# Left-key scores of four heads in one matmul, and a new unit order, in a two-branch attention kernel

## The chip, the cores and the metric

The kernel runs on one core of a Trainium2 chip, as one program. The metric is the time on the device in microseconds; the profile that is quoted comes from one profiled execution of the program.

## The reference, cut to what matters

The output mixes two attention branches of the same input `x` (2048 rows, 512 columns) by a gate of each row. Branch A goes through 64 segments of 32 rows, one after the other: each segment works on its 32 rows and 8 memory rows, and the first 8 rows of its result are the memory of the next segment. The 64 segments are therefore a serial chain. Branch B (`_B_ref`) has four blocks of 512 rows with causal attention inside each and a running memory; nothing in it depends on branch A.

```python
mem = mem0
for s in range(n_seg):                        # 64 segments of seg_len = 32
    xs = x[:, s*seg_len:(s+1)*seg_len, :]
    h = concatenate([mem, xs], axis=1)        # 8 + 32 = 40 rows
    q, k, v = (einsum('btd,dhe->bhte', h, W) for W in (Wq, Wk, Wv))   # 32 heads of 128
    scores = where(mask, einsum('bhqe,bhke->bhqk', q, k) * scale, -1e9)
    o = einsum('bhqk,bhke->bhqe', softmax(scores), v)
    o = einsum('bhte,hed->btd', o, Wo)
    mem = o[:, :M, :]                         # M = 8
    outs.append(o[:, M:, :])
g = sigmoid((x * gate_w).sum(-1))
return g * a + (1 - g) * b                    # a: branch A, b: branch B
```

## The kernel before

All work is recorded first as operations with their dependencies (class `Prog`) and then written out, engine by engine, in the order of recording; waits on semaphores are derived from the dependencies. Each engine thus runs its instructions strictly in the order in which they were recorded.

**Splitting of a segment.** A segment has 40 rows, handled as 32 "main" rows (8 memory rows and the first 24 of its own) and 8 "left" rows (its last 8). K, Q and V of the main rows are made for each segment. Those of the left rows do not depend on the chain and are made for four segments (a group) at once: units whose names begin with `L`. The 32 heads of a segment are handled in two halves, b = 0 and 1, of 16 heads. Within a half, four heads share each of four tiles j: tile j of 32 partitions holds the keys of heads 4j to 4j + 3 of the half, and these stand side by side along the columns. Each head has `LW` = 56 columns in the score bank: 40 for the main keys against all queries, then 16 for left keys against the queries that may see them (the 8 memory rows and the 8 left rows). The left keys of a tile's four heads, 8 each, fill its 32 partitions together (`KTL`); they are multiplied with the queries of all four heads, and the products of one head's keys with another's queries are masked away. `QT_sb` and `KTL` keep heads in pairs: the two members u of a pair are interleaved, element by element.

**The units of a segment**, in the names that the order uses (`s.` in front is the segment, b the half): `K0x K0y V0x ... Q1x Q1y` are projection passes of 8 matmuls of 512 columns (Q1: 16 of 256), `k q v` evacuate them from PSUM, `TK TQ` transpose K and Q on DVE, `qt` copies left queries on POOL, `Z` puts a mask into a score bank by a matmul (L1547), `S` computes scores (`scores`, L1551 to L1571), `X` takes exponentials on ACT (L1575), `Y` applies a mask on DVE, `M` makes the row sums by matmul (L1594), `L` turns them into reciprocals on ACT (L1601, L1604), `N n` multiply them in on DVE and POOL, `PV` multiplies with values (L1625 main, L1636 left), `E0` to `E3` evacuate (L383 on ACT, L385 on DVE), `W0` to `W3` are the out projection (L1362), `hm` turns the eight new memory rows into input of the next segment (L1662 to L1667), `H ws oL` evacuate and store the result.

**Other units.** `L` units make left K, Q, V of a group, `O` and `T` units finish the output rows of a group, `pj pp` project parts of branch B, and `bS bE bP bT` are its scores (L932), exponentials (L953), values (L985) and remaining steps.

**What sets the order.** The text `A_ORDER` (L1058 on) lists all 4509 units; `plan_a` calls them in that order. A `~` behind a unit swaps the engine that evacuates in it: ACT in place of DVE or the other way (`evac`, L383 and L385).

**The scores before.** After 16 matmuls for the main keys (L1561), two loops k and j make eight matmuls for the left keys (L1566): weights are the left keys of tile j (32 columns), moving are the queries of two of its four heads, 32 columns.

Of the kernel before, what the change touches and what calls it, by code (L numbers as in the profile page):

```python
# [867 lines left out]
class BAttn:  # L868
# [195 lines left out]
    1.TQ0 1.TQ1x 1.k1 1.S0~ 1.TK1 1.q1y 1.TQ1y 1.V0x bE 1.S1~ 1.X0 bE 1.X1 1.V0y~ 1.Y0 1.M0 1.v0 1.L0 1.V1x 1.M1 1.L1 1.N0 1.V1y 1.n0 1.n1 1.v1~ 1.N1 pj
    pj bE 1.PV~ 1.E0 1.E1~ L1.VL0x 1.E3 1.E2 bE 1.oL 1.W0 1.W1 1.W2 1.W3 pp~ 1.hm bS 1.H bP bP 2.qt L1.VL0y bE L1.VL0e pj bE 2.K0x 2.K0y~ bT 2.Q0x~ 2.Q0y~
    2.Q1x~ bE bE bP 2.k0 bP 2.TK0 bS 2.q0~ 2.q1x 2.TQ0 2.Q1y~ 2.q1y~ 2.K1x~ 2.TQ1x 2.TQ1y bE 2.K1y~ 2.S0 bE bE 2.X0 1.ws 2.k1~ 2.Z1 2.V1x pj bE 2.V1y~
    2.TK1 2.Y0 2.S1 2.v1 2.M0 pp 2.V0x 2.X1 3.qt bP 2.M1 bS~ bP 2.V0y 2.L0 2.N0 2.L1 2.n1 2.n0 2.N1 pj pj 2.v0 bT bE bE 2.PV pj bE 2.E0 2.W0 2.E1~ 2.E2~
    2.E3~ bE pp~ 2.W1 2.W2 2.W3 2.hm bP 2.H bP bS~ pj pj 3.K0x bE bE bE 3.K0y~ 3.Q0x 3.k0~ 3.Q0y~ 3.K1x bE 3.q0~ 2.ws 3.K1y~ 3.Q1x~ 3.Z1 3.TK0 3.k1 3.q1x
    3.TQ0 3.S0 3.Q1y pp~ 3.V0x~ 3.TK1 3.X0 3.Y0 3.TQ1x 3.q1y bP 3.TQ1y bP 3.M0 3.L0 pj 3.S1~ bS 3.X1 pp~ 3.V0y~ 3.M1 3.V1x~ 3.n0 bE 3.V1y bE 3.L1 3.v0 pj
    3.n1 3.N0 3.v1~ 2.oL bE 3.N1 pj 3.PV~ 3.E0~ L1.VL1x 4.qt 3.E1 L1.VL1y bE 3.W0 3.W1 3.E2 3.W2 3.E3~ 3.W3 L1.VL1e 3.hm pp 3.H bP pj bS~ bP pj L1.VLt  # L1070
    4.K0x bE 4.K0y 4.Q0x~ bT 4.Q0y~ bT bE bE bE 4.k0 4.Q1x~ 4.Q1y 3.ws L2.xl pp~ bP bP 4.K1x 4.TK0 4.q0~ 4.q1x~ 4.TQ0 4.K1y 4.q1y 4.S0 bS 4.TQ1x 4.TQ1y
    4.X0 4.V1x~ 4.k1~ 4.Z1 bE 4.V1y~ 4.TK1 3.oL 4.S1 bE 4.Y0 4.M0 bE 4.v1 4.X1 4.V0x~ 4.L0 4.V0y 4.v0 4.M1 4.L1 4.n0 pj pj 4.N0 4.N1 4.n1 pj 4.PV~ bE pj
    bP 4.E1 4.E0 4.E2~ 4.E3 4.W0 4.W1 4.W2 pp~ 4.W3 bS~ bP O0.0 bE pp~ 4.hm O0.1 5.K0x~ 5.K0y bE 5.Q0x 4.H 5.qt bT 5.k0~ 5.Q0y~ 5.K1x~ bE bE 5.K1y 5.TK0
    5.Z1 5.q0~ 5.TQ0 5.k1~ 5.Q1y 5.TK1 5.q1y 5.TQ1y 5.S0~ 5.X0 5.Q1x~ bP 5.V1x~ 5.q1x 5.V1y~ 4.ws 5.Y0 5.M0 5.TQ1x 5.v1 5.S1~ 5.V0x~ 5.X1 5.V0y~ 5.L0 5.M1
    5.v0 O0.2 5.L1 5.N0 4.oL 5.n0 O0.3 bP 5.N1 5.n1 5.PV L2.KL1x 5.E0~ L2.KL1y O0.e 5.E1~ bS~ O0.s 5.E2~ 5.E3 5.W0 5.W1 bE 5.W2 5.W3 L2.KL0x bE L2.KL1e
    L2.KL0y~ bE bE bS bP 5.hm 5.H 6.qt L2.KL0e~ bP 6.Q1x~ 6.K0x~ 6.Q0x 6.Q0y bE bE 6.K0y 6.q1x~ bE bE 6.Q1y~ 6.TQ1x 6.q0~ 5.oL bS bP bT bP 6.k0~ 6.q1y
    6.K1x~ 6.TQ0 bE 6.TK0 6.K1y~ 6.k1~ 6.S0~ bE bE 6.V1x 6.V1y~ 6.Z1 6.TQ1y 6.TK1 6.X0 6.V0x~ bE 5.ws 6.S1 6.Y0 6.M0 6.X1 6.v1 6.L0 6.V0y 6.M1 6.L1 bP bP
    6.v0 bS 6.n1 6.N0 6.N1 L2.QL1x 6.n0 bE L2.QL1y bE bT 6.PV bE 6.E0 6.E1 6.E2 L2.QL0x 6.E3~ 6.W0 L2.QL1e 6.W1 6.W2 bE 6.W3 bP 7.qt bS 7.Z1 6.hm 6.H bP
    bE L2.QL0y~ bT 7.Q1x~ bE 7.K0x~ 6.ws L2.QL0e 6.oL 7.Q0x~ 7.Q0y 7.K0y 7.q1x 7.TQ1x bE bE 7.K1x 7.k0 7.q0 7.TQ0 7.K1y 7.Q1y bP bP 7.k1 7.TK0 7.S0~ 7.TK1
    bS~ 7.q1y 7.X0 bE 7.V0x~ 7.TQ1y 7.Y0 7.S1~ 7.V0y 7.v0 bE 7.M0 7.V1x~ 7.X1 7.M1 7.L0 7.L1 7.V1y~ 7.N0 L2.VL0x 7.n0 7.v1 7.N1 L2.VL0y L2.VL1x 7.n1 bE  # L1080
    7.PV L2.VL1y bE L2.VL0e bP 7.E2 7.E0~ bT 7.E1~ L2.VL1e~ bP bS~ 7.W0 8.qt 7.E3 bE L2.VLt 7.W1 7.W2 7.W3 bE bE bE 7.hm 7.H bS~ 8.Z1 bP bP bE bT bE 8.Q0x
    bE 8.Q0y 8.q0 8.K0x 8.K0y 8.K1x bE 8.k0 8.K1y 8.k1 8.TQ0 8.Q1y 8.TK0 8.Q1x 8.S0 8.q1y 8.q1x 8.V1x~ 8.TK1 8.X0 8.TQ1y 8.V1y 8.TQ1x 8.Y0 8.S1~ L3.xl
    9.Z1 8.M0 bP 8.v1 8.V0x~ 8.X1 7.oL 8.L0 8.M1 8.L1 8.N0 8.V0y 8.N1 L3.KL1x 7.ws 8.v0~ O1.0 8.n0 8.n1 8.PV~ 8.E0 8.E1~ 8.E3~ L3.KL1y bP 8.E2~ 8.W0 8.W1
    8.W2 L3.KL1e 9.qt 8.W3 bS~ O1.1 bE bE O1.2 8.hm 9.Q0x~ 9.Q0y 8.oL bE bE 9.K0x~ 8.H 9.K0y 9.K1x~ 9.q0 9.K1y~ 9.k0~ 9.TQ0 9.Q1y~ 9.k1 9.q1y 9.TK0 9.Q1x~
    9.TK1 9.TQ1y 9.q1x 9.TQ1x 9.S0 9.X0 9.Y0 9.V1x 9.V1y~ 8.ws 9.S1~ bP 9.X1 9.M0 9.V0x~ 9.L0 9.M1 9.V0y 9.L1 L3.KL0x 9.v1 9.N0 9.n0 9.n1 9.v0~ L3.KL0y
    9.N1 9.PV O1.3 9.E0 bP O1.e 9.W0 9.E1 9.E2~ 9.W1 bT 9.W2 9.E3~ 9.W3 11.Z1 bS 9.hm 10.Z1 10.qt L3.KL0e~ L3.QL0x bE bE bE O1.s bT L3.QL0y~ 10.Q0x 10.K0x
    L3.QL0e 9.H 10.Q0y~ 10.K1x~ 10.q0 10.K0y 10.K1y~ bE 10.TQ0 10.Q1y~ 10.k0 10.Q1x 9.oL 10.TK0 10.k1 10.TK1 10.V1x 10.q1y 10.q1x 10.TQ1y 10.TQ1x 10.S0~
# [151 lines left out]
    T14.b 62.PV~ 62.E0 62.E2 62.W0 63.qt 62.E1 62.E3 62.W1 62.W2 62.oL 62.W3 O15.0 O15.1 62.hm O15.2 O15.3 63.Q0x 63.V0x T14.a 62.H O15.e 63.Q0y 63.K0x
    63.q0 63.K0y 63.TQ0 63.K1x 63.Q1y 63.K1y 63.k0 63.TK0 T14.t 63.S0 62.ws O15.s 63.Q1x~ 63.q1y~ 63.k1~ 63.X0 63.Y0 63.q1x 63.V1x~ 63.M0 T15.l 63.V0y~  # L1240
    63.TK1 63.V1y 63.TQ1x 63.TQ1y 63.S1~ 63.L0 63.v0 63.X1 63.v1~ 63.n0 63.M1 63.L1 T14.f 63.N0 63.n1 T15.b 63.N1 63.PV~ 63.E0 63.E1 63.E3 63.E2 T15.a
    63.W0 63.W1 63.W2 63.W3 T15.t 63.H T15.f
# [534 lines left out]
```

## Time and profile before

| | |
|---|---|
| median of three runs | 830.14 us (827.49 to 831.01) |
| profiled execution, its own time | 830.02 us |
| its span, first to last instruction | 828.3 us |
| TensorE busy (matmuls, lengths modelled) | 788.2 us, 95% |
| DVE, ACT, POOL busy | 71%, 68%, 35% |
| left-key matmuls (L1566) | 1024, mean length 177 ns |
| main-key score matmuls (L1561) | 2048, mean length 182 ns |

In the profile, PE is TensorE's matmuls and PEld its weight loads, which run beside them. Lengths of matmuls overlap, since they are pipelined: what a group of them takes from its successor is the distance from its start to the next group's start. An entry in brackets at a row's end is the time the engine had stood idle, with what released it.

### The profile page before, as it was taken

To read this page: it belongs to the slowest core of one execution; us is meant where nothing else is said; L and a number is where in the kernel's file an instruction comes from. 1 tells how busy PE (TensorE), PEld (TensorE's weight loads), DVE (VectorE), ACT (ScalarE), POOL (GpSimd) and SP (SyncE) were. 2 spreads that over 40 slices of the span, in tenths; PEclk is the share of its full clock that TensorE was granted. 3 is DMA by queue.
4 is the path that set the end of the run, shared out by engine and by line. 5 is a ranking of instruction groups with operands and counts; after the bars stand their busy time and mean duration, and the time that the engine had idled before them with its cause. 6 is when DMAs were issued, how large, how long until landed. Compare 5 with 4: busy or idle time off the path is not lost.

```text
span 828.3 us, 51528 instructions
## 1 busy us (share of the span) xinstructions
PE 788.2 (95%) x23213; PEld 485.5 (59%) x23219; DVE 591.1 (71%) x1483; ACT 560.0 (68%) x1356; POOL 289.1 (35%) x727
## 2 busy tenths in 40 slices
...
PEclk9999999999999999999999999999999999999999
...
DMA packets 100600, 72.34 MB, mean 87 GB/s; under 512 B 58036, under 2 KB 94492, under 8 KB 98844
## 3 DMA queue, kind: packets, MB, share of 16 engines
...
q8 instruction: 182, 2.98, 1.6%
...
## 4 chain that ended last, share of the span: by engine, by line
PE 80%; DVE 9%; ACT 7%; issue 2%; POOL 1%; DMA 0%; DVEq 0%; POOLq 0%
PE ps L1279 38%; PE ps L1362 15%; PE ps L1501 6%; PE ps L698 3%; PE ps L932 2%; PE ps L1625 2%; PE ps L985 2%; ACT PTT L953 2%; PE ps L1594 2%; PE ps L1561 2%; PE ps L1442 1%; DVE oTt L1009 1%; PE ps L717 1%; ACT R_sb L1604 1%; POOL PTT L959 1%
## 5 line engine op out<-in xcount | busy, mean ns | idle before, releaser
L953 ACT ACTIVATE PTT<-ps 128x512 bf16<-128x512 f32 x320 | 173.6, 604 | 49.6 <-PE ps L932 34.9
L959 POOL TENSOR_SCALAR_AFFINE_SELECT PTT<-PTT 128x128 bf16<-128x128 bf16 (+2 forms) x320 | 121.7, 380 | 217.7 <-ACT PTT L953 199.6
L1279 PE MATMUL ps<-Wv_sb,xTp 128*32 128x512 bf16 x2048 | 144.1, 379 | 0.0
L1279 PE MATMUL ps<-Wk_sb,xTp 128*32 128x512 bf16 x2048 | 133.3, 379 | 2.6 <-DVE xTp L1667 2.2
L1362 PE MATMUL ps<-Wo_sb,OT_sb 128*32 128x256 bf16 x4096 | 125.6, 273 | 7.6 <-ACT OT_sb L383 3.7
L1362 PEld LDWEIGHTS ps<-Wo_sb,OT_sb 128*32 128x32 bf16 x4096 | 103.5, 97 | 31.1 <-ACT OT_sb L383 21.8
L1613 POOL TENSOR_TENSOR P_sb<-P_sb,R_sb 128x64 bf16<-128x64 bf16 x128 | 49.9, 390 | 176.0 <-ACT R_sb L1604 171.6
L383 ACT ACTIVATE QN_sb<-ps 128x256 bf16<-128x256 f32 (+1 forms) x155 | 67.2, 439 | 34.0 <-PE ps L1279 29.5
L1279 PEld LDWEIGHTS ps<-Wk_sb,xTp 128*32 128x32 bf16 x2048 | 56.6, 97 | 50.5 <-DVE xTp L1667 7.8
L383 ACT ACTIVATE OT_sb<-ps 128x320 bf16<-128x320 f32 x167 | 62.9, 439 | 30.4 <-PE ps L1636 29.5
L383 ACT ACTIVATE KN_sb<-ps 128x512 bf16<-128x512 f32 x89 | 53.1, 600 | 32.9 <-PE ps L1279 32.6
L385 DVE CAST V_sb<-ps 128x512 bf16<-128x512 f32 x82 | 56.4, 688 | 25.7 <-PE ps L1279 24.0
L1501 PE MATMUL ps<-Wq_sb,xTp 128*32 128x256 bf16 x2048 | 72.0, 273 | 0.8 <-DVE xTp L1667 0.5
L1279 PE MATMUL ps<-Wq_sb,xTp 128*32 128x512 bf16 x1024 | 70.1, 380 | 2.5 <-DVE xTp L1667 2.1
L1291 DVE STREAM_TRANSPOSE QT_sb<-QN_sb 128x128 f32<-128x128 f32 (+1 forms) x192 | 63.0, 335 | 11.1 <-ACT QN_sb L383 9.1
L1291 DVE STREAM_TRANSPOSE KT_sb<-KN_sb 128x256 f32<-128x256 f32 x128 | 55.7, 435 | 14.7 <-ACT KN_sb L383 10.9
L1501 PEld LDWEIGHTS ps<-Wq_sb,xTp 128*32 128x32 bf16 x2048 | 54.4, 97 | 19.8 <-DVE xTp L1667 6.2
L1575 ACT ACTIVATE P_sb<-ps 128x224 bf16<-128x224 f32 x128 | 45.6, 358 | 28.9 <-PE ps L1566 23.6
L1662 DVE STREAM_TRANSPOSE tt<-ps 128x256 f32<-128x256 f32 x63 | 28.3, 449 | 44.2 <-PE ps L1362 43.5
L385 DVE CAST OT_sb<-ps 128x320 bf16<-128x320 f32 x89 | 40.2, 483 | 23.9 <-PE ps L1636 23.7
L1608 DVE TENSOR_TENSOR P_sb<-P_sb,R_sb 128x160 bf16<-128x160 bf16 x128 | 41.0, 331 | 15.8 <-ACT R_sb L1604 15.1
L1279 PEld LDWEIGHTS ps<-Wv_sb,xTp 128*32 128x32 bf16 x2048 | 44.6, 95 | 12.7 <-ACT KN_sb L383 0.7
...
## 6 DMA issues: line engine op xcount, KB each, us to landing
...
```

What stands on the lines that cost most here:

```text
L383: P.op("act", lambda a: a.activation(dst, src, ACT.Copy), reads=[v.rbank[k] for k in bks], writes=dres, name=name)
L385: P.op("dve", lambda d: d.tensor_copy(dst, src), reads=[v.rbank[k] for k in bks], writes=dres, name=name)
L953: P.op("act", lambda a: a.activation(pt, v.pb[bk], ACT.Exp, scale=v.SCALE_B), reads=[v.rbank[bk]], writes=[rp], name="be%d_%d" % (n, t))
L959: P.op("gp", lambda g: g.affine_select(mv, mv, [[0, len(cut)], [1, 128]], ALU.is_ge, 0.0, base=0, channel_multiplier=-1), reads=[rp], writ ...
L1279: ins = pe.matmul(pb[bk][SEG * j:SEG * (j + 1), :], lhs(c), cols(w, j) if split else w[:, 512 * j:512 * (j + 1)], start=(c == 0), stop=(c ...
L1291: P.op("dve", lambda d: d.transpose(to, src), reads=reads, writes=writes, name=name)
L1362: ins = pe.matmul(pb[bk][SEG * j:SEG * (j + 1), 0:256], lhs(h), Wo_sb[:, h, :].rearrange("p (k q c) -> p q k c", q=2, c=64)[:, j % 2], sta ...
L1501: ins = pe.matmul(pb[bk][SEG * j:SEG * (j + 1), 0:256], lhs(c), cols(w_sb[:, c, 2048 * b + 1024 * half:2048 * b + 1024 * (half + 1)], j), ...
L1575: P.op("act", lambda a: a.activation(P_sb[:, b, :], pb[bk][:, 0:So], ACT.Exp, scale=SCALE), reads=[rbank[bk]], writes=[Rs("Pm%d" % b), Rs( ...
L1608: P.op("dve", lambda d: d.tensor_tensor(wide[b][:, :, 0:L], wide[b][:, :, 0:L], R_sb[:, b, :].rearrange("p (i q) -> p i q", q=L), ALU.mult ...
L1613: P.op(ENG["n"], lambda d: d.tensor_tensor(left, left, grp04(R_sb[:, b, :]), ALU.mult), reads=[Rs("R0_%d" % b)], writes=[Rs("PL%d" % b)], ...
L1662: P.op("dve", lambda d: d.transpose(v.tt[:, :, :].rearrange("p (k n) t -> p k n t", n=2), src), reads=[rbank[wb["bk"]]], writes=[Rs("tt")] ...
```

## The change

Two things change. First, in `scores`, the loop over k goes: the left keys of tile j are multiplied with the queries of all four heads in one matmul of 64 columns, so a unit has four such matmuls in place of eight. The queries are now read in the order head pair, position, member of the pair (the two members of a pair are neighbours in `QT_sb`), and so the output is written in that order too: `p (k u w) -> p k w u` puts the member u, `LW` = 56 fp32 columns apart, innermost. Before, each matmul wrote two runs of 16 neighbours.

```diff
-                for k in range(2):
-                    for j in range(4):
-                        m = 8 * b + 2 * j
-                        ins = pe.matmul(heads4(pb[bk][SEG * j:SEG * (j + 1), 0:So])[:, 2 * k:2 * k + 2, L:LW], KTL[par][:, r, m // 2, :, :, :].rearrange("p k m u -> p (k m u)"),
-                                        QT_sb[:, m + k, :, :].rearrange("p (a q) u -> p u a q", q=8)[:, :, 0::4, :],
-                                        start=new, stop=True, skip_group_check=True)
+                for j in range(4):
+                    m = 8 * b + 2 * j
+                    lefts = pb[bk][SEG * j:SEG * (j + 1), 0:So].rearrange("p (k u w) -> p k w u", u=2, w=LW)[:, :, L:LW, :]
+                    ins = pe.matmul(lefts, KTL[par][:, r, m // 2, :, :, :].rearrange("p k m u -> p (k m u)"),
+                                    QT_sb[:, m:m + 2, :, :].rearrange("p k (a q) u -> p k a (q u)", q=8)[:, :, 0::4, :],
+                                    start=new, stop=True, skip_group_check=True)
```

Second, `A_ORDER` is another list of the same 4509 units; the number of each unit stays. Some `~` marks move as well. One line of it, from segment 0:

```diff
-    0.k0~ wl wl bP L1.xl L1.KL0x L1.KL1x 0.V1y~ L0.QL0e~ 0.TQ1x 0.Z1 wl 0.qt 0.S1~ wl 0.TK0 L1.KL1y~ 0.S0 0.v1~ L1.QL1x L1.KL0y~ L1.QL1y L0.VLt wl wl pp
+    0.k0~ wl wl bP L1.xl L1.KL0x L1.KL1x 0.V1y~ L0.QL0e~ 0.TQ1x 0.Z1 wl 0.qt 0.TK0 L1.KL1y L1.KL0y pj 0.S1 wl L0.VLt 0.X1 wl 0.S0 0.v1 L1.KL1e L1.KL0e~
```

Place one: TensorE in segment 0, from the last V pass to the row sums. L1547 is the mask, L1561 and L1566 are the scores of one half, L1594 the sums, `Wk_sb,xL` and `Wq_sb,xL` passes for left rows of group 1, L836 a pass of branch B. Before:

```order
L1279 MATMUL ps<-Wv_sb,xTp 32x512 x8
L1547 MATMUL ps<-mbias,id 32x224 x4
L1561 MATMUL ps<-QT_sb,KT_sb 32x40 x16
L1566 MATMUL ps<-QT_sb,KTL 32x2x16 x8
L1279 MATMUL ps<-Wk_sb,xL 32x512 x8
L1561 MATMUL ps<-QT_sb,KT_sb 32x40 x16
L1566 MATMUL ps<-QT_sb,KTL 32x2x16 x8
L1279 MATMUL ps<-Wq_sb,xL 32x512 x8
L1279 MATMUL ps<-Wk_sb,xL 32x512 x8
L1279 MATMUL ps<-Wq_sb,xL 32x512 x8
L1594 MATMUL ps<-P_sb,onesb 32x160 x4
```

The same place in the changed kernel:

```order
L1279 MATMUL ps<-Wv_sb,xTp 32x512 x8
L1547 MATMUL ps<-mbias,id 32x224 x4
L1279 MATMUL ps<-Wk_sb,xL 32x512 x16
L836 MATMUL ps<-woB_sb,xTp 32x512 x8
L1561 MATMUL ps<-QT_sb,KT_sb 32x40 x16
L1566 MATMUL ps<-QT_sb,KTL 32x2x16x2 x4
L1561 MATMUL ps<-QT_sb,KT_sb 32x40 x16
L1566 MATMUL ps<-QT_sb,KTL 32x2x16x2 x4
L1594 MATMUL ps<-P_sb,onesb 32x160 x4
```

Three passes now stand ahead of the first scores that stood behind them or further on; the two score groups follow each other, and the sums of the first come right behind. Left-key groups are four matmuls in place of eight.

Place two: TensorE in segment 19, from its last V pass over the values (L1625, L1636) to the out projection (L1362). L932 is a score step of branch B, L985 one of its value steps. Before:

```order
L1279 MATMUL ps<-Wv_sb,xTp 32x512 x8
L932 MATMUL ps<-KQj 128x256 x8
L1625 MATMUL ps<-P_sb,V_sb 128x40 x32
L1636 MATMUL ps<-P_sb,VL 128x4x2x8 x8
L1279 MATMUL ps<-Wk_sb,xL 32x512 x8
L1362 MATMUL ps<-Wo_sb,OT_sb 32x256 x64
L1279 MATMUL ps<-Wk_sb,xL 32x512 x8
```

In the changed kernel:

```order
L1594 MATMUL ps<-P_sb,onesb 32x160 x4
L1594 MATMUL ps<-P_sb,onesb 32x4x2x8 x4
L985 MATMUL ps<-PTT,Vj 32x256 x8
L932 MATMUL ps<-KQj 128x256 x8
L1625 MATMUL ps<-P_sb,V_sb 128x40 x32
L1636 MATMUL ps<-P_sb,VL 128x4x2x8 x8
L1362 MATMUL ps<-Wo_sb,OT_sb 32x256 x64
L1279 MATMUL ps<-Wk_sb,xL 32x512 x8
```

The projection pass for left rows between values and out projection has gone behind the out projection; a value step of branch B now stands ahead of the values in place of the last V pass, which lies one group earlier. Such moves run through the whole program.

More of the change, by code (lines that the diff above doesn't have):

```diff
@@ L1064 @@
[L1064 to L1087, printed above, removed]
@@ L1239 @@
[L1239 to L1242, printed above, removed]
+    15.k1 15.q1y 15.TK0 15.q1x 15.TK1 15.S0~ 15.V0x~ 15.X0 15.TQ1y 15.TQ1x 14.oL 15.V0y 15.Y0 15.S1~ bP 15.M0 15.X1 bP 15.V1x~ bT 15.M1 15.L0 15.L1 14.ws
@@ new lines @@
+    17.Z1 bE bE 17.Q0x~ bE 17.Q0y 17.K0x~ 17.K0y~ 17.q0~ 17.TQ0 17.K1x 17.k0~ 17.K1y~ 17.Q1x 17.TK0 T2.t 16.H~ bE 17.Q1y~ 17.k1 17.q1x 17.q1y 17.S0
+    17.V0x~ 17.TK1 17.TQ1x 17.X0 16.ws 17.TQ1y 17.V0y 17.S1~ 17.Y0 17.v0 bP 17.X1 17.M0 17.V1x 17.L0 17.M1 17.V1y 17.L1 L5.QL0x L5.QL0y~ 18.Z1 17.v1~
+    17.n0 17.N0 17.n1 17.N1 16.oL 17.PV~ bP L5.VL0x L5.QL0e 17.E0 17.E1~ 17.W0 17.W1 17.E3~ 17.E2~ 17.W2 bT 17.W3 17.hm O3.0 18.qt bT L5.VL0y O3.1 18.K0x
+    18.K0y~ 18.Q0x 18.Q0y~ 18.K1x L5.VL0e~ 18.K1y 18.k0~ 18.Q1x~ 18.TK0 18.q0~ 18.TQ0 18.k1 18.TK1 18.Q1y~ 18.S0~ 18.V1x 18.q1x 18.TQ1x 18.q1y 18.V1y~
@@ new lines @@
+    21.K1x~ 21.K1y~ 21.TQ0 21.Q1x bP 21.S0~ O4.e~ bP 21.k1 21.q1x O4.s bS 21.V1x 21.TK1 21.TQ1x 20.oL 21.Z1 21.X0 21.S1 bE 21.Y0 T2.f 21.M0 bE 21.X1
+    21.V1y 21.L0 21.V0x~ 21.M1 21.V0y 21.v1 21.n0 21.N0 21.L1 21.N1 21.v0~ 21.n1 L6.VL0x 21.PV bE 21.E3 L6.VL0y 21.E0 21.E2~ 21.W0 L6.VL0e 21.E1~ bE 21.W1
+    21.W2 21.W3 21.hm bS~ bP 22.qt bP 22.Z1 L6.QL0x 21.H 22.Q0x bE 22.K0x 22.Q0y 22.K0y~ bT bE 22.q0 bE bE 22.K1x 22.TQ0 22.k0 22.K1y~ 22.Q1y~ 22.TK0
+    22.Q1x~ 22.k1 22.q1y 22.q1x 22.S0 22.TK1 22.V0x 22.V1x~ 22.TQ1y 22.TQ1x 22.X0 22.S1 22.Y0 23.Z1 22.X1 22.M0 22.L0 22.V1y 22.v1 22.N0 21.oL 22.M1
@@ new lines @@
+    29.M0 28.ws 29.V0y 29.X1 29.v0 29.M1 29.L0 L8.QL0x 29.n0 29.N0 L8.QL0y bP 30.Z1 29.L1 29.n1 29.N1 29.PV L8.QL0e 29.E0 30.qt 29.E2~ 29.E1~ bT 29.W0
+    29.W1 29.E3~ 29.W2 29.W3 bS~ bP bE 29.hm O6.1 bE bE bE O6.2 30.K0x 30.K0y 30.k0 30.Q0x 30.TK0 30.Q0y 30.q0~ 30.TQ0 30.K1x~ 30.K1y 30.Q1x~ 30.Q1y~
+    30.k1 30.q1x 30.S0 30.V0x~ 30.q1y 30.V0y 30.TK1 30.X0 30.TQ1x 30.TQ1y 30.Y0 30.S1 29.oL 30.X1 30.M0 30.V1x~ 30.M1 30.v0 30.V1y L8.VL0x 30.L0 30.N0
+    30.n0 L8.VL0y 30.L1 30.n1 30.v1~ 30.N1 31.qt 30.PV O6.3 30.E0 30.E3 30.E1~ bP 30.W0 30.E2~ 30.W1 O6.e 30.W2 30.W3 L8.QL1x L8.VL1x L8.VL1y 31.Z1
@@ new lines @@
+    32.k1 32.S0 32.TK1 32.q1y 32.X0 32.TQ1y 32.V1x 32.V0x~ 32.S1~ 32.Y0 bP 32.M0 31.ws L9.KL0e~ 32.X1 32.L0 32.V1y~ 32.M1 32.n0 32.L1 32.v1 32.V0y T6.l
+    32.N0 32.N1 32.v0~ 32.n1 bT O7.0 O7.1 32.PV 32.E0 32.E1~ 32.W0 32.E3 32.E2 32.W1 32.W2 32.W3 bS~ 32.hm O7.2 O7.3 bE 33.qt bE 32.H~ bE 33.K0x~ 32.ws
+    33.Q0x bE 33.Q0y T6.a 33.q0 33.K0y~ 33.K1x 33.K1y 33.k0 33.TQ0 33.k1 O7.e 33.TK0 bP 33.Q1y 33.S0 33.q1y~ 33.X0 33.TK1 33.TQ1y 33.Q1x bP bS 33.q1x
+    33.V1x 33.Y0 33.TQ1x 33.M0 bE bE 33.S1 33.V1y 33.X1 33.L0 33.V0x~ 33.n0 33.v1 33.M1 33.L1 33.V0y 33.n1 33.v0~ L9.QL0x 32.oL bE 33.N0 L9.QL0y 33.N1
@@ new lines @@
+    33.PV~ 33.E0 33.E1 34.qt L9.KL1x 33.E2~ 33.E3 33.W0 33.W1 33.W2 33.oL bE 33.W3 O7.s 33.hm bP L9.QL0e bP bS~ 33.H bE L9.KL1y~ 34.Q0x 34.Q0y~ 34.K0x
+    34.K0y bE 34.q0~ 34.K1x 34.K1y~ bT 34.k0~ 34.Q1y~ bE bE 34.Q1x 34.TK0 33.ws 34.V0x~ 34.TQ0 34.k1 34.TK1 34.Z1 34.S0~ 34.V1x~ 34.q1y 34.TQ1y 34.q1x
+    34.X0 34.TQ1x 34.Y0 34.S1~ 34.V0y 34.X1 34.M0 34.V1y~ 34.v0 34.L0 34.M1 34.v1 34.L1 34.n0 T6.b L9.VL0x 34.n1 34.N0 34.N1 34.PV L9.KL1e~ 34.E0 bP bP
+    34.E1 34.E2 bT 34.W0 T6.t 34.W1 34.W2 34.E3~ 34.W3 bS~ L9.QL1x 34.hm bE 34.H L9.QL1y~ bE 35.Z1 35.Q0x~ bE bE 35.Q0y~ L9.QL1e 35.K0x~ 35.q0 35.qt
@@ new lines @@
+    L11.KL1y 40.n0 40.N0 40.N1 40.v0~ L11.KL1e~ 40.n1 40.PV bS~ 40.E1~ bP bP T7.f 40.E0 40.E3 40.W0 40.W1 39.ws 40.E2 40.W2 bE bE 40.W3 bT L11.KL0x
+    L11.KL0y~ bE bE bS 41.qt bP bP 40.hm 41.K0x bT L11.KL0e~ 41.K0y~ bE 41.Q1x bE 41.Q0x~ 40.H 41.q1x~ 41.Q0y bE 41.q0 41.K1x~ 41.k0 41.K1y 41.Q1y~
+    41.V1x~ 41.TK0 41.TQ0 41.TQ1x 41.S0~ bE 40.ws 41.k1 41.q1y 40.oL 41.TK1 41.TQ1y 41.X0 41.V1y 41.Z1 41.v1~ bP 41.S1 41.Y0 bP 41.M0 41.V0x~ 41.X1 41.L0
+    41.M1 bT 41.n0 41.N0 41.L1 bS~ 41.n1 41.N1 41.V0y bE bE 41.v0 L11.QL0x 41.PV L11.QL0y bE 41.E0 bE 41.E1 bT 41.E2 41.W0 41.E3~ 41.W1 41.W2 41.W3 bP
@@ new lines @@
+    47.V1x~ 47.q1x 47.TQ1y 47.TQ1x 47.S1~ 47.X0 47.Y0 T9.a 47.M0 47.X1 47.V0y L12.QL1e 48.Z1 47.M1 47.L0 47.v0 47.n0 47.L1 47.N0 47.V1y 47.n1 L13.KL0x
+    47.v1~ 47.N1 47.PV~ 47.E0 L13.KL0y~ 47.E1 bP 47.W0 47.W1 47.E2~ 48.qt 47.E3 47.W2 47.W3 bS~ bP L13.KL0e~ T9.b 47.hm bE bE 48.Q0x~ 47.H T9.t 48.Q0y
+    48.K0x 48.K0y~ 48.K1x 48.k0~ 48.q0~ bE 48.TQ0 48.K1y~ 48.Q1x~ 48.Q1y~ 48.k1 48.TK0 47.oL 48.q1x 48.TK1 48.S0 48.q1y 48.V1x~ 48.X0 bE 48.TQ1x 48.V1y
+    48.TQ1y 48.S1 48.Y0 48.X1 48.v1 49.Z1 48.M0 48.V0x~ 48.L0 48.M1 47.ws 48.V0y~ L13.KL1x 48.N0 48.n0 48.L1 O11.0 48.v0~ 48.n1 48.N1 48.PV bP L13.KL1y
@@ new lines @@
+    58.q1x~ 58.S0~ 58.q1y 58.V1x 58.TK1 58.TQ1x 58.X0 58.V1y~ 58.TQ1y O13.s 58.Z1 58.S1~ 58.Y0 57.H~ bP 58.v1 58.M0 bP 58.V0x 59.qt 58.X1 57.ws 58.M1
+    58.L0 58.V0y~ 58.n0 58.L1 58.N0 58.v0~ 58.N1 58.n1 bT L15.QL1x L15.VL1x 58.PV L15.QL1y~ bT 58.E0 58.E1~ 58.E2 58.W0 58.E3~ 58.W1 58.W2 58.W3 L15.VL0x
+    L15.VL1y 58.hm L15.VL0y 59.Z1 59.Q0x 59.K0x~ 59.K0y~ 59.Q0y 59.K1x 59.K1y~ 58.H~ 59.Q1x~ L15.VL0e~ L15.VL1e bT 59.k0~ 59.q0~ 59.TQ0 59.Q1y 59.k1
+    59.TK0 59.TK1 59.q1x 59.S0 59.V0x~ 59.V0y~ 59.q1y 59.TQ1x 59.TQ1y 59.X0 59.S1 59.Y0 59.X1 58.oL 58.ws 59.v0 59.M0 59.V1x 59.M1 59.L0 59.N0 59.n0
@@ new lines @@
+    61.K1x 60.H~ 61.K1y~ 61.k1 61.Q1x 61.q0 61.TK0 61.q1x 61.TQ0 61.Q1y 61.S0 61.V0x~ 61.q1y 61.X0 61.TK1 61.TQ1x 61.TQ1y 61.V1x 61.S1~ 61.Y0 61.X1 61.M0
+    60.ws 61.V0y~ 61.v0 61.M1 61.V1y 61.L0 61.n0 61.N0 61.L1 61.n1 61.v1~ 61.N1 T13.b 61.PV~ O14.3 61.E3 61.E0 61.E2 61.E1 O14.e T13.a 61.W0 61.W1 O14.s
+    T13.t 61.W2 61.W3 T14.b 61.oL 62.qt 62.Z1 61.hm 62.Q0x 62.K0x 62.K0y T13.f 62.Q0y~ 62.k0~ 62.q0~ 62.K1x~ 62.K1y 62.Q1y 61.H~ 62.Q1x 62.TK0 62.k1
+    62.TQ0 62.TK1 62.S0~ 62.q1y 62.V1x 62.TQ1y 62.q1x 62.V0x 62.X0 62.TQ1x 62.S1~ 62.X1 T14.l 62.Y0 62.M0 62.V1y 61.ws 62.v1 62.L0 63.qt 62.N0 62.M1
```

293 lines of the change are left out of this document (142 added, 151 removed).

## The prediction

> **What bounds the kernel now.** I read the page first, then the waits of TensorE, then stretches of the timeline. The page: shares of the span by engine, granted clock per slice, and the chain that ended last.
>
> ```profile
> span 828.3 us, 51528 instructions
> PE 788.2 (95%) x23213; PEld 485.5 (59%) x23219; DVE 591.1 (71%) x1483; ACT 560.0 (68%) x1356; POOL 289.1 (35%) x727
> PEclk9999999999999999999999999999999999999999
> PE 80%; DVE 9%; ACT 7%; issue 2%; POOL 1%; DMA 0%; DVEq 0%; POOLq 0%
> ```
>
> TensorE is busy for 95% of the span and carries 80% of the chain; the clock is full in every slice. So time leaves this kernel in two ways only: a matmul that TensorE need not stream, or a wait of TensorE that gets shorter. DVE (71%) and ACT (68%) are in the chain with 9% and 7%: each where TensorE had run out of other work. The profiled execution took 830.02 us, 1.7 us more than its span; the median of the three runs shown is 830.14, so sums made against 830.02 hold for it too.
>
> Next, the waits of TensorE's weight loads, longest in total first (us, times, longest one). A weight load is pulled ahead of the stream, so these rows overstate what the array lost; the 40.1 us between span and busy time understates it.
>
> ```profile
> PEld ps L1362 <- ACT OT_sb L383: 21.8, 55, 0.7
> PEld ps L1625 <- ACT V_sb L383: 21.5, 39, 1.2
> PEld ps L1594 <- ACT P_sb L1575: 17.1, 47, 0.6
> PEld ps L1279 <- DVE xTp L1667: 14.7, 33, 1.4
> PEld ps L1561 <- DVE QT_sb L1291: 14.7, 51, 0.4
> PEld ps L932 <- issue: 12.2, 46, 1.1
> ```
>
> These are the joints of one segment's chain: scores wait for transposed queries (L1561), sums for the exponentials (L1594), values (L1625) for evacuated V and the normalised weights, the out projection (L1362) for evacuated attention output, the next segment (L1279) for the new memory rows. Half a microsecond each, in 64 segments: small waits with other passes laid between. Which passes lie there is what the unit order decides.
>
> **Part 1: one matmul for four heads.** Two score units of segment 2 and what stands around them on TensorE (start, length, group):
>
> ```profile
> 91.87 0.27 PE L1561 MATMUL ps<-QT_sb,KT_sb 128*32 128x40 bf16 x16
> 91.97 0.21 PE L1566 MATMUL ps<-QT_sb,KTL 128*32 128x32 bf16 x8
> 92.02 0.27 PE L1547 MATMUL ps<-mbias,id 128*32 128x224 bf16 x4
> 92.11 0.60 PE L1279 MATMUL ps<-Wv_sb,xTp 128*32 128x512 bf16 x8
> 92.55 0.60 PE L836 MATMUL ps<-xTp,woB_sb 128*32 128x512 bf16 x8
> ...
> 93.51 0.21 PE L1566 MATMUL ps<-QT_sb,KTL 128*32 128x32 bf16 x8
> 93.56 0.28 PE L1594 MATMUL ps<-P_sb,onesb 128*32 128x160 bf16 x8
> 93.66 0.63 PE L1279 MATMUL ps<-Wv_sb,xTp 128*32 128x512 bf16 x8
> ```
>
> The lengths include the pipeline; what the path pays is the distance from start to start. Eight 512-column matmuls take 0.44 us (92.11 to 92.55): 4096 columns, 0.107 ns each, four 32-column tiles side by side. Eight left-key matmuls take 0.05 us in both places, where 256 columns at that rate are 0.027: with 32 columns they are too short to run at the column rate and cost about 6 ns apiece. The L1594 row holds four matmuls of 160 columns and four of 64 (896 columns); it takes 0.10 us, and 896 x 0.107 ns = 0.096: at 64 columns the column rate already holds.
>
> After the change a unit has four matmuls of 64 columns, so 0.027 us in place of 0.050: 0.023 saved, times 128 units (1024 matmuls in the group row below, 8 a unit) = 2.9 us. TensorE streams on before and after the unit, so this comes off the path whole, except where the engine then sits waiting for the exponentials anyway: 47 of the 128 sums do (L1594 row above), which at worst hands back 47 x 0.023 = 1.1 us. They wait for an exponential that starts when the scores end, so most of these get earlier too; I keep 2.9 and take 1.8 as the low end. The 512 weight loads that go were hidden: no idle stands before this line's.
>
> ```profile
> L1566 PE MATMUL ps<-QT_sb,KTL 128*32 128x32 bf16 x1024 | 27.9, 177 | 0.0
> L1566 PEld LDWEIGHTS ps<-QT_sb,KTL 128*32 128x32 bf16 x1024 | 17.1, 93 | 0.0
> ```
>
> One thing the trace does not show. The new matmul writes head pairs innermost: consecutive results land 56 fp32 apart, where every matmul of these rows writes runs of at least eight neighbours. Its price is bounded below by the 0.027 us of unbroken writing. Above I take four times that, 0.107 us, as an estimate: the four tiles' results, now stored side by side, would go one tile after the other. I use the lower end, since the nearest row in size, the 64-column half of L1594, runs at the column rate with its output in pieces of eight.
>
> [...]
>
> **Part 2: the new unit order.** All counts of units stay; only their order and which of ACT and DVE takes some evacuations change (seven more of the attention outputs go to DVE, for instance). Evacuations that change engine cost little, by these rows of the same copy on both:
>
> ```profile
> L383 ACT ACTIVATE OT_sb<-ps 128x320 bf16<-128x320 f32 x167 | 62.9, 439 | 30.4 <-PE ps L1636 29.5
> L385 DVE CAST OT_sb<-ps 128x320 bf16<-128x320 f32 x89 | 40.2, 483 | 23.9 <-PE ps L1636 23.7
> ```
>
> Seven times 44 ns is 0.3 us on engines with a quarter of the span free: nothing.
>
> Place one, segment 0. Before, the score unit followed the bias directly and waited:
>
> ```profile
> 64.50 0.27 PE L1547 MATMUL ps<-mbias,id 128*32 128x224 bf16 x4
> 65.59 0.28 PE L1561 MATMUL ps<-QT_sb,KT_sb 128*32 128x40 bf16 x16 [0.82 <-DVE KT_sb L1291]
> 65.59 0.17 PEld L1561 LDWEIGHTS ps<-QT_sb,KT_sb 128*32 128x32 bf16 x16 [1.20 <-POOL QT_sb L1714]
> ```
>
> Now three passes of 8 x 512 columns (3 x 0.44 us) stand between: the wait of 0.82 us is covered. In exchange the first sums follow the scores directly.
>
> Place two, segment 19. Before, a projection pass covered the evacuation between values and out projection; now nothing does. A covered and an uncovered case in the old trace:
>
> ```profile
> 302.53 0.26 PE L1636 MATMUL ps<-P_sb,VL 32*128 32x64 bf16 x8
> 302.72 0.61 PE L1279 MATMUL ps<-Wk_sb,xL 128*32 128x512 bf16 x8
> 303.51 1.93 PE L1362 MATMUL ps<-Wo_sb,OT_sb 128*32 128x256 bf16 x64 [0.17 <-ACT OT_sb L383]
> ...
> 821.12 0.26 PE L1636 MATMUL ps<-P_sb,VL 32*128 32x64 bf16 x8
> 821.45 0.77 ACT L383 ACTIVATE OT_sb<-ps 128x320 bf16<-128x320 f32 x2 [1.05 <-PE ps L1636]
> 821.94 0.12 PEld L1362 LDWEIGHTS ps<-Wo_sb,OT_sb 128*32 128x32 bf16 x8 [0.68 <-ACT OT_sb L383]
> ```
>
> In both, the out projection starts 0.8 to 1.0 us after the left values, so an uncovered place loses what a pass would have filled, 0.44 us. Counting rows of the whole program, values followed directly by the out projection stand 5 times before and 7 times now: + 0.9 us. Scores followed directly by sums stand 28 times and now 30: 2 x 0.36 (17.1 us over 47 waits) = + 0.7. With the 0.8 of place one, the counted joints come to + 0.8 us. On SP the stores of out-projection rows and the loads of the second attention's keys change places early in the queue; who waits for those loads is L932 (12.2 us in all, above), and the score steps of that attention stand as far apart as before, so I put that at nothing, with a share of the 12.2 in the spread below.
>
> The rest of the order cannot be costed place by place. As an estimate of its spread: about two joints a segment, 128 in all, each changed by up to one pass either way, 0.44 us; changes without a common sign add up as the root, 0.44 x 11.3 = 5 us.
>
> The sum: 830.0 - 2.9 + 0.8 = 827.9 us, give or take 5 for the order.
>
> **Rivals.**
>
> Strided stores at half the column rate. For it: each new result lies in another place than its neighbour, and no row here does that. The unit's left part is then 0.054 us: 128 x 0.027 = 3.4 us over the forecast, 831.3. [...]
>
> Strided stores much slower, the case on the other side. Place: the 128 left-key groups, in the middle of a streaming TensorE, with no cover. At four times the column time the group is 0.107 us, 0.080 over the forecast: 128 x 0.080 = 10.2 us, 838.1. It decides from 0.076 us a group on, where 128 x 0.049 = 6.3 us brings the time to 834.2. [...]
>
> The order shortens waits in earnest. The array is idle for at least 40.1 us, most of it at the joints of the six rows; an order that fills a seventh of that takes 6 us off the forecast: 822. For it: each of these places has a pass that could lie better. Against it: the counts above found no such shift.
>
> The merge does nothing: were its saving swallowed by waits everywhere, the time would be the order's alone, 830.8, and its chance is in the spread of the forecast. Against it: in 81 of 128 cases nothing waits behind the scores.
>
> **How the numbers follow.** Forecast 0.50, half rate 0.25, much slower 0.10, shorter waits 0.15. A measurement of this kernel tells about 0.5% (4.2 us) from no change, so faster is below 825.9 and slower above 834.2. With a spread of 5 us about each case: the forecast gives 0.34 / 0.56 / 0.10 for faster, same, slower; half rate 0.13 / 0.60 / 0.27; much slower 0 / 0.2 / 0.8; shorter waits 0.8 / 0.2 / 0. Weighted: 0.32, 0.48, 0.20. The range leaves out a tenth at each end of the mixture: 820.5 to 837. The likeliest case by itself spans 821.5 to 834.3.
>
> **What would show it.** Right: L1566 with 512 matmuls and a distance to the next group of about 0.03 us; TensorE waits in the six rows of the same total within 5 us; segment 0's first scores without a wait; an idle before L1362 in segment 19 of 0.7. Wrong: a distance of 0.05 (half rate) or over 0.07; or a wait row that moved by more than 5 us, which would be the order and not the merge.

## The result, and the profile after

| | before | changed |
|---|---|---|
| median, same chip | 831.23 us | 828.01 us |
| ratio | | 0.9965, 95% interval 0.9951 to 0.9979 |
| profiled execution, its own time | 830.02 us | 827.52 us |

By the ratio the change makes the kernel 0.35% faster, 2.9 us of 830; the two medians differ by 3.2 us. The forecast was 827.9, 2.1 us under its base of 830.0. The number came out; the mechanism behind its largest term did so only in part.

The page of the changed kernel: span, busy time by engine, chain by engine.

```profile
span 825.8 us, 50495 instructions
PE 786.9 (95%) x22701; PEld 486.5 (59%) x22707; DVE 587.9 (71%) x1485; ACT 562.0 (68%) x1354; POOL 288.0 (35%) x727
PE 80%; ACT 6%; DVE 6%; DMA 3%; POOL 2%; issue 2%; SPq 1%; ACTq 0%; DVEq 0%; POOLq 0%
```

TensorE has 512 matmuls fewer and as large a share of span and chain as before. Span less busy time was 40.1 us and is 38.9. The waits of TensorE's weight loads (us, times, longest), the six rows of the prediction:

```profile
PEld ps L1362 <- ACT OT_sb L383: 23.4, 58, 0.8
PEld ps L1625 <- ACT V_sb L383: 19.8, 38, 1.2
PEld ps L1594 <- ACT P_sb L1575: 16.9, 52, 0.6
PEld ps L1561 <- DVE QT_sb L1291: 14.7, 50, 0.5
PEld ps L1279 <- DVE xTp L1667: 13.8, 38, 1.6
PEld ps L932 <- issue: 10.4, 40, 1.5
```

Together 99.0 us, against 102.0 before; none moved by more than 2. The wait ahead of the out projection (L1362) grew, as did the number of waits for exponentials (L1594). The groups of the left-key matmuls (busy us, mean ns of one, idle before):

```profile
L1566 PE MATMUL ps<-QT_sb,KTL 128*32 128x64 bf16 x512 | 29.5, 217 | 0.0
L1566 PEld LDWEIGHTS ps<-QT_sb,KTL 128*32 128x32 bf16 x512 | 13.8, 93 | 0.0
```

Half as many matmuls, but each is 40 ns longer than before (217 against 177), and their busy time is higher, not lower (29.5 us against 27.9). The two places of the change, segment 0 first, on TensorE's timeline:

```profile
64.78 0.27 PE L1547 MATMUL ps<-mbias,id 128*32 128x224 bf16 x4
64.88 1.04 PE L1279 MATMUL ps<-Wk_sb,xL 128*32 128x512 bf16 x16
65.74 0.60 PE L836 MATMUL ps<-woB_sb,xTp 128*32 128x512 bf16 x8
66.17 0.27 PE L1561 MATMUL ps<-QT_sb,KT_sb 128*32 128x40 bf16 x16
...
66.43 0.25 PE L1566 MATMUL ps<-QT_sb,KTL 128*32 128x64 bf16 x4
66.97 0.28 PE L1594 MATMUL ps<-P_sb,onesb 128*32 128x160 bf16 x8 [0.29 <-ACT P_sb L1575]
...
301.11 0.23 PE L1566 MATMUL ps<-QT_sb,KTL 128*32 128x64 bf16 x4
301.13 0.63 PE L1279 MATMUL ps<-Wv_sb,xTp 128*32 128x512 bf16 x8
301.59 0.27 PE L1594 MATMUL ps<-P_sb,onesb 128*32 128x160 bf16 x8
...
304.24 0.26 PE L1636 MATMUL ps<-P_sb,VL 32*128 32x64 bf16 x8
305.06 1.93 PE L1362 MATMUL ps<-Wo_sb,OT_sb 128*32 128x256 bf16 x64 [0.57 <-ACT OT_sb L383]
```

In segment 0 the first scores (66.17) start without their wait, and the sums now wait 0.29. In segment 19 the uncovered out projection waits 0.57. In between (301.11 to 301.59) is the row to remember: the left keys take 0.02 us to the start of the next pass, about as forecast (the median over such places is 0.028), but that pass of eight matmuls then takes 0.46 us where such a pass took 0.44 before.

### The profile page after: what moved, and what is told of

Same layout as the page of the kernel before. It is cut to its first block, busy times and chain, and to the rows that moved or that the text cites. A ratio compares the mean times of both kernels' runs of the same rounds, so it can differ in the third digit from the quotient of the medians.

```text
span 825.8 us, 50495 instructions
## 1 busy us (share of the span) xinstructions
PE 786.9 (95%) x22701; PEld 486.5 (59%) x22707; DVE 587.9 (71%) x1485; ACT 562.0 (68%) x1354; POOL 288.0 (35%) x727
## 3 DMA queue, kind: packets, MB, share of 16 engines
q8 instruction: 178, 2.92, 1.5%
## 4 chain that ended last, share of the span: by engine, by line
PE 80%; ACT 6%; DVE 6%; DMA 3%; POOL 2%; issue 2%; SPq 1%; ACTq 0%; DVEq 0%; POOLq 0%
PE ps L1279 38%; PE ps L1362 16%; PE ps L1501 6%; PE ps L1625 3%; PE ps L932 3%; PE ps L985 2%; PE ps L698 2%; POOL PTT L959 2%; PE ps L1561 1%; ACT PTT L953 1%; PE ps L1594 1%; DMA Wv_sb<-in_A_Wv_dram 1%; PE ps L1442 1%; ACT R_sb L1604 1%; PE ps L836 1%
## 5 line engine op out<-in xcount | busy, mean ns | idle before, releaser
L1279 PE MATMUL ps<-Wv_sb,xTp 128*32 128x512 bf16 x2048 | 144.3, 383 | 0.0
L1362 PE MATMUL ps<-Wo_sb,OT_sb 128*32 128x256 bf16 x4096 | 126.2, 275 | 7.8 <-ACT OT_sb L383 5.1
L1279 PE MATMUL ps<-Wk_sb,xTp 128*32 128x512 bf16 x2048 | 131.5, 379 | 2.0 <-DVE xTp L1667 1.9
L1362 PEld LDWEIGHTS ps<-Wo_sb,OT_sb 128*32 128x32 bf16 x4096 | 104.6, 97 | 30.8 <-ACT OT_sb L383 23.4
L1279 PEld LDWEIGHTS ps<-Wk_sb,xTp 128*32 128x32 bf16 x2048 | 56.4, 97 | 51.4 <-DVE xTp L1667 7.0
L383 ACT ACTIVATE KN_sb<-ps 128x512 bf16<-128x512 f32 x95 | 57.0, 601 | 35.0 <-PE ps L1279 34.3
L383 ACT ACTIVATE QN_sb<-ps 128x256 bf16<-128x256 f32 (+1 forms) x148 | 63.8, 437 | 24.6 <-PE ps L1279 18.5
L383 ACT ACTIVATE OT_sb<-ps 128x320 bf16<-128x320 f32 x160 | 60.2, 438 | 28.7 <-PE ps L1636 28.2
L1279 PE MATMUL ps<-Wq_sb,xTp 128*32 128x512 bf16 x1024 | 70.0, 380 | 1.0 <-DVE xTp L1667 0.9
L385 DVE CAST OT_sb<-ps 128x320 bf16<-128x320 f32 x96 | 43.3, 485 | 23.9 <-PE ps L1636 23.3
L1279 PEld LDWEIGHTS ps<-Wv_sb,xTp 128*32 128x32 bf16 x2048 | 44.2, 100 | 14.6 <-ACT QN_sb L383 1.0
L1608 DVE TENSOR_TENSOR P_sb<-P_sb,R_sb 128x160 bf16<-128x160 bf16 x128 | 40.1, 329 | 12.2 <-ACT R_sb L1604 11.3
```

Of the source, the lines that this page charges most:

```text
L383: P.op("act", lambda a: a.activation(dst, src, ACT.Copy), reads=[v.rbank[k] for k in bks], writes=dres, name=name)
L385: P.op("dve", lambda d: d.tensor_copy(dst, src), reads=[v.rbank[k] for k in bks], writes=dres, name=name)
L1279: ins = pe.matmul(pb[bk][SEG * j:SEG * (j + 1), :], lhs(c), cols(w, j) if split else w[:, 512 * j:512 * (j + 1)], start=(c == 0), stop=(c ...
L1362: ins = pe.matmul(pb[bk][SEG * j:SEG * (j + 1), 0:256], lhs(h), Wo_sb[:, h, :].rearrange("p (k q c) -> p q k c", q=2, c=64)[:, j % 2], sta ...
L1608: P.op("dve", lambda d: d.tensor_tensor(wide[b][:, :, 0:L], wide[b][:, :, 0:L], R_sb[:, b, :].rearrange("p (i q) -> p i q", q=L), ALU.mult ...
```

## The experiments

Two theories at the start. A: as forecast, the merge pays in TensorE's stream and the order costs a little. B: the strided stores run at half the column rate, so the merge pays nothing in the stream, and the order or the waits pay. Ratios are to the kernel before on the same chip: e1 to e4 ran on one chip, e5 to e8 on a second, e9 to e12 on a third.

| run | code, order | ratio (95%) | profiled, us |
|---|---|---|---|
| e1, e6 | merged, old order | 1.000 (0.9981 to 1.0018), 1.0002 (0.9983 to 1.002) | 834.74, 830.03 |
| e2, e7 | split, new order | 1.000 (0.9982 to 1.0018), 1.0004 (0.9987 to 1.0021) | 834.0, 832.49 |
| e5 | merged, new order | 0.9962 (0.9944 to 0.9979) | 826.68 |
| e3 | neighbouring stores, new order | 0.9956 (0.9929 to 0.9982) | 827.9 |
| e4 | paired columns, new order | 0.995 (0.9931 to 0.9969) | 827.98 |
| e8 | paired columns, old order | 0.999 (0.9968 to 1.0011) | 829.2 |
| e9, e10 | merged, new order, moved by 42, 98 | 0.9963 (0.9945 to 0.9981), 0.997 (0.9953 to 0.9986) | 827.18, 828.87 |
| e11, e12 | split, new order, moved by 42, 98 | 1.0016 (0.9998 to 1.0034), 1.001 (0.9997 to 1.0024) | 830.12, 830.95 |

**Each part alone, e1 and e2.** e1 is the kernel before with the edit of `scores` only; e2 has the new `A_ORDER` and `~` marks with the old loops over k and j.

> The unit order of before, with the left-key matmuls merged. Theory A (the step of the prediction: the strided results are written at the column rate, 0.027 us a group): 2.9 us faster than before, ratio 0.9965. Theory B (they are written at half that rate, 0.054 us a group, and the shortfall shows only in the group behind them): 128 x 0.004 = 0.5 us slower to no change, ratio 0.9995 to 1.001.

> The new unit order, with the left-key matmuls split as before. Theory A: the order gives 0.8 us more than before, and with the saving of 2.9 missing the ratio is 1.001. Theory B: the whole measured gain is the order's, 3 us less than before, ratio 0.996, the same as the changed kernel.

Both parts alone measured nothing: 1.000 each, with an error of 0.18%, so a gain or a loss of up to 1.5 us isn't excluded for either. Yet the two together are 0.35% faster. Neither theory has that: a merge that is worth nothing and an order that is worth nothing should add up to nothing. The merged matmul looks the same in the old order, by the groups of e1:

```profile
L1566 PE MATMUL ps<-QT_sb,KTL 128*32 128x64 bf16 x512 | 29.6, 216 | 0.8 <-issue 0.8
```

**Neighbouring stores, e3.** The changed kernel with the results of the merged matmul written as two runs of 32 neighbours. Left-key scores then lie in other columns than their heads'; the amount of work is the same.

```diff
-lefts = pb[bk][..., 0:So].rearrange("p (k u w) -> p k w u", u=2, w=LW)[:, :, L:LW, :]
+lefts = pb[bk][..., 0:So].rearrange("p (k x) -> p k x", k=2)[:, :, L:L + 32]
```

> The changed kernel, but each merged matmul writes its 64 results as two runs of 32 neighbours; everything else as in the changed kernel. The left-key scores then stand in wrong columns, so the output is not the reference's; the instructions and their sizes are the same. Theory A: same time as the changed kernel, 0.9965 of before, and an L1566 length as in the changed kernel. Theory B: 128 x 0.027 = 3.4 us less than the changed kernel, ratio to before 0.9925, and L1566 shorter by 25 ns, at the 192 ns of the other 64-column matmuls.

The group of e3 first, then segment 19 on its timeline, to be held against 301.11 to 301.59 above.

```profile
L1566 PE MATMUL ps<-QT_sb,KTL 128*32 128x64 bf16 x512 | 26.1, 190 | 0.0
```

```profile
300.40 0.20 PE L1566 MATMUL ps<-QT_sb,KTL 128*32 128x64 bf16 x4
300.43 0.60 PE L1279 MATMUL ps<-Wv_sb,xTp 128*32 128x512 bf16 x8
300.86 0.27 PE L1594 MATMUL ps<-P_sb,onesb 128*32 128x160 bf16 x8
```

With neighbouring stores the matmul is 190 ns long in place of 217 (the profile models these lengths; the starts behind them it doesn't), and the pass behind it takes 0.43 us in place of 0.46. So the strided write does cost time, and it is paid by the group behind. Taken over all V passes that follow left keys without a wait (48 or more in each kernel), the median start of that pass's second set of four matmuls, counted from the start of the left keys, is 0.265 us before, 0.268 changed, 0.268 in e1 and 0.243 in e3. The extra 0.025 us on the 0.028 that the matmuls themselves take makes 0.053 us a unit, against 0.050 split. That is the half rate of theory B, though with one size measured a fixed cost of 25 ns a group would look the same. The merge therefore costs TensorE's stream some 128 x 0.003 = 0.4 us, and neighbouring stores free 128 x 0.025 = 3.2 us. But e3 as a whole stands at 0.9956, within the changed kernel's interval, where theory B had 0.9925: most of those 3.2 us did not reach the end.

**A layout in which the stores are neighbours, e4.** Each head pair has its 80 main columns first and then its 32 left columns with the members alternating; masks, sums, normalisation and values read by the new layout. This computes all that the changed kernel does.

```diff
+c0 = lambda i: 112 * (i // 2) + L * (i % 2)          # main columns of head i
+pairs = lambda ap: ap.rearrange("p (k z) -> p k z", k=2)
-lefts = pb[bk][..., 0:So].rearrange("p (k u w) -> p k w u", u=2, w=LW)[:, :, L:LW, :]
+lefts = pairs(pb[bk][..., 0:So])[:, :, 2 * L:112]
```

> The changed kernel with another column layout of the score bank and the weights: for each pair of heads 2 x 40 main columns and then 32 left columns in which the two members alternate, so that the merged matmul writes neighbours and the result stays the reference's. The sums and left values then read their moving operand at a step of two elements, and the left normalisation on POOL runs at that step. Theory A: same as the changed kernel or slower by what the stepped reads cost. Theory B: 3.4 us less than the changed kernel (0.9925 of before) if the stepped reads are free, which the left-key matmuls of before, with the same step, suggest; the normalisation on POOL may eat some of it.

The matmul itself answers to the layout as in e3 (two lines lower in this code):

```profile
L1568 PE MATMUL ps<-QT_sb,KTL 128*32 128x64 bf16 x512 | 25.9, 190 | 0.0
```

Its ratio of 0.995 (0.9931 to 0.9969) is 0.15% under the changed kernel's 0.9965, inside the error; the changed kernel itself was not run on this chip. So of the 3.2 us some 0.8 (e3) and 1.3 us (e4) show. Where the rest went is not shown. It is not in the six rows of waits, which sum to 97.0 us in e3 and 96.9 in e4, less than the 99.0 of the changed kernel. In the single executions that were profiled, stalls of TensorE without a releaser are longer, 6.9 and 6.7 us against 3.8 (3.6 to 5.9 in the other three profiles of the merged matmul in this order); the last experiments look at these.

**The same again, e5 to e7, and the paired columns in the old order, e8.** The changed kernel and its two halves once more, now side by side on another chip, since the result of e1 and e2 fitted no theory.

> The changed kernel again, on the chip of the next three. Open is whether 0.9965 holds beside kernels that have each half of the change alone. If the halves add up (merge 1.000, order 1.000), it should now come out at 1.000; if the first result stands, 0.995 to 0.998.

> The merge in the unit order of before, again. Strided stores at half rate: 0.5 us more work than before less what 1024 fewer instructions save, ratio 1.000 within 0.002. If the merge is worth something by itself: below 0.998.

> The new order with the split matmuls, again. If the order carries the gain: 0.996 to 0.998. If order and merge help only together: 1.000 again.

> The merge with the column layout in which its results are neighbours, in the unit order of before. Against the merge alone it takes 128 x 0.027 = 3.4 us of store time away, in the place that the prediction had costed: 0.9965 of before if TensorE's time counts whole (the 2.9 us of the prediction), near 1.000 if the saving is swallowed by waits further on in an order that was made for longer groups.

The pattern held on the second chip: both 0.9962, merge alone 1.0002, order alone 1.0004. e8, with the results side by side (its left-key matmuls 190 ns long, as in e4), came to 0.999 in the old order, not the 0.9965 of a saving that counts whole. So it is not an accident of one chip: merge and order together are worth more than the sum of what each is worth alone, and what the merge is worth in the old order, if anything, is too small for these runs to tell.

**Where the instruction blocks end, e9 to e12.** Some stalls of TensorE have no releaser in the trace; here are two of the changed kernel's, on its timeline, each in the middle of an out projection.

```profile
319.19 0.95 PE L1362 MATMUL ps<-Wo_sb,OTL 128*32 128x256 bf16 x28 [0.33 <-issue]
...
389.74 0.29 PE L1362 MATMUL ps<-Wo_sb,OT_sb 128*32 128x256 bf16 x2 [0.97 <-issue]
```

Counting TensorE's instructions from the first (weight loads, matmuls and semaphore instructions), 155 of the 157 such stalls in all fourteen traces stand at one place, numbers 186 to 199 of every 256, and no other period from 200 to 330 gathers them like that. (Some traces lack six or seven records, which moves the count by as much.) The page's rows of the instruction queues fit:

```profile
q8 instruction: 178, 2.92, 1.5%
q14 instruction: 38, 0.31, 0.1%
```

Together they moved 3.23 MB for the 50495 instructions of the page, 64 bytes each; 2.92 MB in 178 packets is 16.4 KB a packet, so 256 instructions. In the profiled executions TensorE's idle time without a releaser sums to 3.8 and 3.6 us in the changed kernel and its repetition, 6.3 before, 10.1 and 6.7 in e1 and e6, 8.5 and 5.8 in e2 and e7. Most of it stands ahead of out projections; the row of the changed kernel first, then that of e2:

```profile
PE ps L1362 <- issue: 3.0, 5, 1.0
```

```profile
PE ps L1362 <- issue: 6.8, 9, 1.2
```

The expectations below go by a wider count of the same stalls, with larger sums. The merge takes away eight instructions a unit and so moves the ends of blocks against the work; a third theory was that the gain comes from where they fall. To move them alone, the seven warm-up matmuls at the start were cut into more and shorter ones of the same 3584 columns: 28 of 128 (42 more instructions) or 56 of 64 (98 more).

```diff
-WARM = 7
+WARM = 28
-ins = pe.matmul(v.pb[bk], v.warm[:, 0:128], v.warm[:, :], start=True, stop=True)
+ins = pe.matmul(v.pb[bk][:, 0:128], v.warm[:, 0:128], v.warm[:, 0:128], start=True, stop=True)
```

> The changed kernel with its seven warm-up matmuls of 512 columns split into 28 of 128, which moves all later TensorE instructions by 42 places against the blocks of 256 in which they are fetched, with no other work. Fetch theory (the gain of the whole change comes from where the fetch stalls fall, 6.8 us in all in it against 8.5 to 13 in the other kernels): the stalls at block ends go to 8.5 us or more and the ratio to 0.998 to 1.003. Wait theory (the new order with the shorter left part meets its evacuations better): the stalls may change, the ratio stays 0.995 to 0.998 and the waits of weight loads stay near 171 us.

> The same with 56 warm-up matmuls of 64 columns: a move by 98 places. Fetch theory: another draw, ratio between 0.996 and 1.003, not equal to that of the move by 42 and following the sum of the stalls at block ends. Wait theory: 0.995 to 0.998 again.

> The new order with the split left-key matmuls, moved by 42 places. Fetch theory: ratio between 0.996 and 1.002, following the stalls at block ends. Wait theory: 0.9985 to 1.002 as unmoved, so that the merge is worth 0.3% in this order at this place too.

> The new order with the split left-key matmuls, moved by 98 places. Fetch theory: ratio between 0.996 and 1.002, following the stalls at block ends. Wait theory: 0.9985 to 1.002, and the merge worth 0.3% against the changed kernel moved by 98.

The stalls stayed at the same instruction numbers (186 to 188 of 256, but for two), so they belong to the place in the block and not to the operation; their sums were 5.9, 4.1, 4.7 and 4.3 us. The ratios didn't follow: the changed kernel kept 0.9963 and 0.997, the split one stayed at 1.0016 and 1.001, though it had no more of these stalls (4.7 and 4.3 us) than the changed one (5.9 and 4.1). The theory of the block ends falls as the cause of the gain. It may have a part in the scatter of single executions: e1 and e6 are the same kernel, 4.7 us apart in their profiled runs, with 3.4 us of difference in these stalls; but e2 and e7 differ by 2.7 in the stalls and by 1.5 in time.

What the runs then say together: split less merged in the new order is 830.2 - 826.64 = 3.6 us on the second chip (e7, e5), and 831.02 - 825.99 = 5.0 (e11, e9) and 830.79 - 827.22 = 3.6 us (e12, e10) on the third, some 4 us. In the old order it is nothing, twice, give or take 1.5 us.

One part of it is seen. The wait of the row sums for the exponentials, with the same moved start, split (e11) and then merged (e9):

```profile
PEld ps L1594 <- ACT P_sb L1575: 17.4, 50, 0.6
```

```profile
PEld ps L1594 <- ACT P_sb L1575: 16.4, 51, 0.6
```

Over four traces each the mean is 17.6 split and 16.5 merged: 1.2 us over 51 waits, 0.023 us each, the forecast's saving per unit, at just those joints where the exponentials are waited for. The starts agree, and they don't hang on modelled lengths: at the 52 places where the sums wait for them in all eight traces, the exponentials start 0.321 us after the left keys in place of 0.349, and the sums 0.761 us after them in place of 0.782, 1.1 us in all. In the old order it is there as well, by the waits of before (17.1, shown above) and of e1:

```profile
PEld ps L1594 <- ACT P_sb L1575: 15.9, 46, 0.6
```

By the starts it is 0.766 us there in place of 0.788. The rest of the 4 us in the new order is not traced to a place. The waits for the next segment's input (L1279 for `xTp`) are 1.2 us shorter on average over the four traces (14.0 against 15.2, with a scatter as large). Stalls without a releaser are 1.5 us shorter (4.4 against 5.8), but that comes from e2 and e7 alone; in the moved kernels, which show the same gain, they are 0.5 us longer with the merge (5.0 against 4.5). The lead grows along the chain: on average over the four traces of each, the values of segment 24 start 1.2 us earlier with the merge, those of the last 4.2. Whether the old order keeps the 1.1 us of its sums, which its error would hide, and why the new one adds some 3 us to them, stays open.

## Why the prediction was right or wrong

- **The time**: 827.9 forecast, 828.0 measured as the median and 827.52 in the profiled execution. That close an agreement is chance: the kernel before had a median of 831.23 beside it, not the 830.0 that the sum starts from, so the change forecast was - 2.1 us and the one measured - 2.9 by the ratio.
- **The 2.9 us of the merge** is the step that failed as a mechanism. "I use the lower end", the column rate, on the ground that the 64-column half of the sums runs at it with pieces of eight. The strided store took about twice that, 0.053 us where the rival had 0.054. So at the 81 units where nothing waits behind the scores, which the prediction counted as sure, the merge saves nothing. At the 47 where the sums wait, whose 1.1 us it was ready to give up, the saving came: "they wait for an exponential that starts when the scores end, so most of these get earlier too" is the part of the reasoning that held. The nearest row in size was not the nearest in what mattered, since its writes had neighbours. The criterion was unsafe too: the distance from L1566 to the next group was 0.028 us, as forecast for the column rate, and the delay sat in the group behind it. Only the length of the matmul (217 against 190) and the pass behind showed it.
- **The rival of half rate** had the price right and the total wrong: its 831.3 adds 0.4 us for the merge and 0.8 for the order to 830.0, and the changed kernel came to 828.0. No row of before shows its factor of a half, which was the author's estimate; the runs showed about two between strided and neighbouring stores (0.053 against 0.028 us), and neighbours brought the matmul from 217 to 190 ns. Not every break between results cost that: the sums' results in pieces of eight ran at the column rate (896 columns in 0.10 us).
- **Four times slower**: no run shows this factor, which was an estimate; the same rows refute it, with 0.053 us a group and not 0.107.
- **The order's + 0.8 us** agrees with the runs but is not shown by them: the four runs of the split kernel in the new order have a mean ratio of 1.0007, + 0.6 us, with an error as large. Its places came out: segment 0's wait of 0.82 went, segment 19 waits 0.57 where 0.7 was said. In the totals, waits for the out projection's input rose by 1.6 us (+ 0.9 said), those for exponentials from 17.1 to 17.6 us with split matmuls (+ 0.7 said).
- **That terms of a stream and of an order add up**: this unstated step failed. The sum treats 0.023 us a unit as leaving the path in any order. The merge measured 0 in the old order and some 4 us in the new, and 3.2 us less of stream in e3 and e4 brought 0.8 and 1.3 us. That the total agrees with the sum is therefore partly luck: the stream saved nothing, the waits of the sums gave 1.1 us, and the rest of the merge's gain in the new order has no place that the runs show.
- **The rival "the order shortens waits in earnest"**: not by itself (1.0007).
- **The rival "the merge does nothing"**: its 830.8 is what the new order gives without the merge; with the merge, 828.0. In the old order the measurement agrees with it.
